# Forty warming matmuls of 32 columns in place of five of 256 columns, ahead of a retention layer and two MLPs

## The chip, the core and the metric

The kernel runs on one core of one Trainium2 chip. The metric is the device time of one execution in microseconds (us). Three runs of the kernel before took 884.5, 882.04 and 884.17 us, with a median of 884.17 us. One more execution was profiled: it took 882.56 us, and its span, from its first to its last instruction, is 880.8 us.

## The reference

The input is a set of queries, keys and values for 4 batches, 8 heads, 576 positions and a head size of 64. Three layers follow one another, all in float32:

```python
scores = q @ k.T / 8                              # per batch and head
ret    = scores * where(i >= j, gamma[h] ** (i - j), 0)
x      = (ret @ v) heads side by side             # 2304 tokens x 512
h      = x @ w_in                                 # 512 x 2048
x      = (h * sigmoid(h)) @ w_out                 # 2048 x 512
h      = x @ w2_in
out    = (max(h, 0) ** 2) @ w2_out
```

The first two lines are a retention layer (attention with a decaying mask in place of the softmax); the two pairs of matrix products behind it are MLPs with the same sizes and different gates.

## The kernel before, in words

The 2304 tokens are cut into 18 units of 128 tokens for the retention layer and into five blocks of 512, 384, 384, 512 and 512 tokens for the MLPs. A unit is two chunks of 64 positions. The retention is computed chunk by chunk with a running state of 64 x 64 per head: for each unit, `scores` makes the products of queries and keys (line 257) and the products of keys and values that go into the state (line 262); `mask` multiplies the first by the decay (line 266, on VectorE); `new_state` adds to the state (lines 295 and 297, on VectorE) and lets GpSimd decay it (line 301); `scale_q` scales the queries on GpSimd (line 274); `prep_k` scales the keys, one half on GpSimd (line 244) and one half on ScalarE (line 247); `values` makes the output from the state and the masked scores (lines 312 to 328), and ScalarE copies a part of it out (line 330). Its matmuls are plain float32 with a tile of 64 x 64, and each is two instructions in the trace, with a weight load (`LDWEIGHTS`) each.

The MLP matmuls (`mm3`, line 74) split every number into a high and a low part and multiply three of the four pairs, in fp32r, one instruction and one weight load each. The weights come in over SyncE's queue and are split by ScalarE and VectorE (`conv_a` to `conv_d`, lines 101 to 125).

The order on each engine is the order in which the program is written; nothing reorders it. At the front, `first_units` writes out by hand how the first four retention units and the split of the first weights interleave on all engines. The first MLP matmul needs units 0 to 2, that is, the low part that line 350 makes of unit 2's output. Behind it stands one long loop of MLP work in which the other 14 units of the retention are spread.

Ahead of `first_units`, the kernel sets a tile `zero` to zero on GpSimd (line 535), takes a PSUM tile `warm`, and multiplies zeros by zeros `WARM` times into it (lines 537 and 538). Nothing reads `warm`. These matmuls stand first in TensorE's queue; the first `scores` stands right behind them and waits for its input, which SyncE's queue begins to load at 0.74 us. The weight tile of a warming matmul is 128 x 128, and its moving tile is 256 columns wide.

Of the kernel before, what the change touches and what calls it, by code (L numbers as in the profile page):

```python
# [31 lines left out]
W2_LAG, W2_NUM, W2_DEN = 0, 9, 8  # L32
HALF = (slice(0, 64), slice(64, 128))
RAW = 3
WARM = 5


@with_exitstack
def kernel(
# [16 lines left out]
    nc = tc.nc  # L56
# [12 lines left out]
    mm = nc.tensor.matmul  # L69
# [135 lines left out]
    def att_psum(startup, name):  # L205
        pool, tag = ps_a, "a"
        if startup:
            pool, tag = [(ps_a, "a"), (ps_s, "s"), (ps_s, "s"), (ps_s, "s")][ps_n[0] % 4]
            ps_n[0] += 1
        return pool.tile([128, 2, 512], F32, tag=tag, name=name)  # L210
# [321 lines left out]
    nb = len(BLOCKS)  # L532
    u_end = [sum(BLOCKS[: j + 1]) // C for j in range(nb)]
    zero = wp.tile([128, 1024], F32, tag="w", name="zero")
    nc.gpsimd.memset(zero[:, 0:256], 0.0)
    warm = att_psum(True, "warm")
    for _ in range(WARM):
        mm(warm[:, 0, 0:256], zero[:, 0:128], zero[:, 0:256], start=True, stop=True)
    nc.vector.memset(dummy, 0.0)
    nc.scalar.activation(dummy, dummy, ACTF.Silu)  # L540
    load_consts(0)
# [129 lines left out]
```

## Time and profile before

| what | value |
|---|---|
| median of three runs | 884.17 us |
| the profiled execution | 882.56 us |
| its span | 880.8 us |
| TensorE busy with matmuls | 857.8 us, 97% of the span, 5954 instructions |
| VectorE, ScalarE, GpSimd busy | 43%, 41%, 6% |
| mean granted TensorE clock | 0.988 of full |

The engines are PE (TensorE's matmuls), PEld (its weight loads, which overlap matmuls), DVE (VectorE), ACT (ScalarE), POOL (GpSimd) and SP (SyncE, whose queue issues most transfers). A granted clock of 1.00 is 2.4 GHz and 0.50 is 1.2 GHz; before the first event of the clock on record the views show 1.00 all the same. Busy times of matmuls are modelled, since matmuls are pipelined: the distance from one start to the next (called the pitch below) tells more than the duration of one. In rows with several instructions merged, the second number is the time from the start of the first to the end of the last.

### The profile page before, as it was taken

The numbers are of one execution on the slowest core, as the hardware profiler recorded it, in microseconds if no ns is written. First come the engines' busy times: TensorE is split into PE (matmuls) and PEld (weight loads), VectorE is DVE, ScalarE is ACT, GpSimd is POOL, SyncE is SP. The second block draws the span as 40 slices with busy tenths as digits, with TensorE's granted clock in tenths as the row PEclk, the third lists the DMA queues.
The fourth block names the chain that finished last, engine by engine and source line by source line (L and its number), as shares of the span: only waits on it lengthen the run. The fifth ranks groups of instructions, "written<-read, shape, count | busy, mean of one in ns | idle before, by whom it ended". The sixth has DMA issues, their size and how long they took to land.

```text
span 880.8 us, 14140 instructions
## 1 busy us (share of the span) xinstructions
PE 857.8 (97%) x5954; PEld 741.2 (84%) x5954; DVE 379.2 (43%) x642; ACT 357.0 (41%) x722; POOL 50.3 (6%) x73
## 2 busy tenths in 40 slices
PE   6799999999999999999999999999999999999998
PEld 5777778999999888888888888899999888888886
DVE  5699992221322222215666777432233332323222
ACT  4588872333334333326565656322222222222221
POOL 4211101000210111000000000000000000000000
PEclk7999999999999999999999999999999999999999
DMA  9455641111211213004433542020020010001001
GB/s 352 148 169 206 217 144 48 49 49 49 85 49 52 82 49 121 1 1 152 136 96 104 180 129 78 0 84 1 1 84 1 1 67 17 1 1 48 1 1 48
DMA packets 21663, 68.27 MB, mean 78 GB/s; under 512 B 2400, under 2 KB 4192, under 8 KB 21216
## 3 DMA queue, kind: packets, MB, share of 16 engines
q1 hardware_dynamic: 16272, 54.14, 17.8%
q10 hardware_dynamic: 5328, 13.24, 4.2%
q8 instruction: 46, 0.75, 0.4%
q14 instruction: 17, 0.14, 0.1%
HBM read 57.93 MB, written 9.44 MB: 76 GB/s over the span
## 4 chain that ended last, share of the span: by engine, by line
PE 84%; DVE 0%; DMA 0%; ACT 0%; issue 0%; SPq 0%
PE acc L74 41%; PE ph L74 40%; PE Q L312 2%; PE P L257 1%; PE P L262 1%; DMA raw<-att 0%; ACT raw L247 0%; DVE gl L466 0%; PE Q L328 0%; DVE Q L345 0%; DVE xl L350 0%; DVE wl L125 0%; ACT xh L348 0%; ACT wh L121 0%; DVE y L508 0%
## 5 line engine op out<-in xcount | busy, mean ns | idle before, releaser
L74 PE MATMUL ph<-xh,wh 128*128 128x512 f32 (+2 forms) x648 | 239.2, 369 | 4.9 <-ACT xh L348 1.9
L74 PE MATMUL ph<-xl,wh 128*128 128x512 f32 (+2 forms) x648 | 237.6, 367 | 0.3 <-DVE xl L350 0.3
L74 PE MATMUL ph<-xh,wl 128*128 128x512 f32 (+2 forms) x648 | 237.8, 367 | 0.0
L466 DVE TENSOR_TENSOR gl<-sg,gh 128x512 fp32r<-128x512 f32 (+1 forms) x160 | 101.8, 637 | 185.2 <-ACT gh L465 185.2
L74 PEld LDWEIGHTS ph<-xh,wh 128*128 128x128 f32 x648 | 121.9, 188 | 22.9 <-ACT sg L458 2.3
L461 DVE SCALAR_TENSOR_TENSOR sg<-ph,sg 128x512 f32<-128x512 f32 (+1 forms) x80 | 51.0, 638 | 198.4 <-ACT sg L460 198.4
L74 PEld LDWEIGHTS ph<-xl,wh 128*128 128x128 f32 x648 | 122.0, 188 | 16.4 <-DVE xl L350 0.5
L74 PEld LDWEIGHTS ph<-xh,wl 128*128 128x128 f32 x648 | 122.0, 188 | 14.7
L460 ACT ACTIVATE sg<-ph 128x512 f32<-128x512 f32 (+1 forms) x80 | 44.5, 556 | 211.7 <-PE ph L74 210.9
L74 PE MATMUL acc<-gh,wh 128*128 128x512 f32 (+1 forms) x320 | 119.5, 374 | 0.0
L74 PE MATMUL acc<-gl,wh 128*128 128x512 f32 (+1 forms) x320 | 117.9, 369 | 0.9 <-DVE gl L466 0.9
L74 PE MATMUL acc<-gh,wl 128*128 128x512 f32 (+1 forms) x320 | 117.7, 368 | 0.0
L458 ACT ACTIVATE sg<-ph 128x512 f32<-128x512 f32 (+1 forms) x80 | 44.3, 554 | 179.3 <-PE ph L74 178.6
L465 ACT CAST gh<-sg 128x512 fp32r<-128x512 f32 (+1 forms) x160 | 92.3, 577 | 53.2 <-DVE sg L461 50.6
L74 PE MATMUL acc<-wh,gl 128*128 128x512 f32 x288 | 112.7, 391 | 0.0
L74 PE MATMUL acc<-wl,gh 128*128 128x512 f32 x288 | 112.6, 391 | 0.0
L74 PE MATMUL acc<-wh,gh 128*128 128x512 f32 x288 | 112.0, 389 | 0.0
L74 PEld LDWEIGHTS acc<-gl,wh 128*128 128x128 f32 x320 | 60.2, 188 | 8.8 <-DVE gl L466 1.5
L74 PEld LDWEIGHTS acc<-gh,wh 128*128 128x128 f32 x320 | 60.3, 188 | 8.5
L74 PEld LDWEIGHTS acc<-gh,wl 128*128 128x128 f32 x320 | 60.2, 188 | 7.5
L74 PEld LDWEIGHTS acc<-wh,gl 128*128 128x128 f32 x288 | 54.0, 188 | 11.4
L74 PEld LDWEIGHTS acc<-wh,gh 128*128 128x128 f32 x288 | 54.1, 188 | 10.5
(50 smaller groups left out, 697.1 us busy)
## 6 DMA issues: line engine op xcount, KB each, us to landing
wr<-w SPq DMA_DIRECT2D x64, 512.0 KB, 3.5
raw<-att SPq DMA_DIRECT2D x32, 512.0 KB, 4.5
x<-y ACTq DMA_DIRECT2D x12, 256.0 KB, 4.3
xr<-x ACTq DMA_DIRECT2D x3, 1024.0 KB, 4.9
out<-y SPq DMA_DIRECT2D x10, 256.0 KB, 2.2
out<-y ACTq DMA_DIRECT2D x7, 256.0 KB, 2.3
x<-y ACTq DMA_DIRECT2D x8, 192.0 KB, 1.9
xr<-x ACTq DMA_DIRECT2D x2, 768.0 KB, 4.3
```

Of the source, the lines that this page charges most:

```text
L74: mm(o, a, b, start=first and i == 0, stop=last and i == n - 1)
L257: mm(o, dims(u, a, e, b, 768), dims(u, a, e, b, 0), start=True, stop=True)
L262: mm(o, toks(u, a, e, b, 256), toks(u, a, e, b, 512), start=True, stop=True)
L312: mm(w, a, b, start=e not in started, stop=last)
L458: nc.scalar.activation(s, ph, ACTF.Silu)
L460: nc.scalar.activation(s, ph, ACTF.Relu)
L461: nc.vector.scalar_tensor_tensor(s, ph, 0.0, s, op0=ALU.max, op1=ALU.mult)
L465: nc.scalar.copy(gh, s)
L466: later.append(lambda: nc.vector.tensor_sub(gl, s, gh))
```

## The change

The count of warming matmuls goes from 5 to 40 and the columns of each from 256 to 32. The memset ahead of them covers 128 columns, those that the weight tile needs, in place of 256. Nothing else differs.

```diff
-WARM = 5
+WARM = 40
...
     zero = wp.tile([128, 1024], F32, tag="w", name="zero")
-    nc.gpsimd.memset(zero[:, 0:256], 0.0)
+    nc.gpsimd.memset(zero[:, 0:128], 0.0)
     warm = att_psum(True, "warm")
     for _ in range(WARM):
-        mm(warm[:, 0, 0:256], zero[:, 0:128], zero[:, 0:256], start=True, stop=True)
+        mm(warm[:, 0, 0:32], zero[:, 0:128], zero[:, 0:32], start=True, stop=True)
```

## Rows read from the trace of the kernel before

**Rows 1.** The page: busy time by engine; chain that ended last, by engine.

```profile
PE 857.8 (97%) x5954; PEld 741.2 (84%) x5954; DVE 379.2 (43%) x642; ACT 357.0 (41%) x722; POOL 50.3 (6%) x73
...
PE 84%; DVE 0%; DMA 0%; ACT 0%; issue 0%; SPq 0%
```

**Rows 2.** Busy time in four stretches from 40 to 120 us, their sum.

```profile
sum 80.00, PE 77.15 PEld 61.64 DVE 73.01 ACT 65.34 POOL 8.48; mean PE 19.29 PEld 15.41 DVE 18.25 ACT 16.34 POOL 2.12
```

**Rows 3.** Timeline of the front: start, length, engine, line, operation, idle before it and releaser.

```profile
1.10 4.57 PE L538 MATMUL warm<-zero 128*128 128x256 f32 x10 [1.10 <-POOL zero L535]
...
6.72 0.81 PE L257 MATMUL P<-raw 64*64 64x64 f32 x32 [1.05 <-DMA raw<-att]
...
9.89 1.48 PE L262 MATMUL P<-raw 64*64 64x64 f32 x32 [2.37 <-POOL raw L244]
...
12.54 0.68 DVE L266 TENSOR_TENSOR rf<-P,cs 128x512 f32<-128x512 f32 x1
...
14.94 0.99 DVE L109 SCALAR_TENSOR_TENSOR t<-wr,t 128x512 int32<-128x512 int32 x1
...
15.85 0.41 DVE L297 TENSOR_TENSOR S<-P,dS 128x256 f32<-128x256 f32 x1
...
16.91 1.86 POOL L274 TENSOR_TENSOR raw<-raw,cs 128x256 f32<-128x256 f32 x2
...
18.74 0.61 POOL L244 TENSOR_TENSOR raw<-raw,cs 128x256 f32<-128x256 f32 x1
...
19.40 1.35 PE L262 MATMUL P<-raw 64*64 64x64 f32 x30 [1.16 <-POOL raw L244]
...
23.14 0.37 ACT L330 COPY xs<-Q 128x256 f32<-128x256 f32 x1 [3.14 <-PE Q L328]
...
25.05 0.43 DVE L107 TENSOR_SCALAR t<-t 128x512 int32<-128x512 int32 x1 [3.12 <-ACT t L101]
...
33.45 0.41 PE L74 MATMUL ph<-xh,wh 128*128 128x384 f32 x1 [1.53 <-DVE xl L350]
```

**Rows 4.** Two stretches of the front: length, busy by engine, PEclk, DMA share, GB/s.

```profile
15.30:18.30 3.00, 2.94 (x110) 2.75 (x102) 2.52 (x5) 0.89 (x2) 2.04 (x4) 0.50 1.02 406
...
19.40:23.10 3.70, 3.70 (x119) 3.64 (x121) 2.12 (x5) 0.60 (x3) 3.01 (x5) 0.57 1.03 411
```

**Rows 5.** The tile warm: shortest, median, longest duration in ns, first and last start.

```profile
L538 PEld LDWEIGHTS warm<-zero x10: 285/337/337, 1.1 to 4.7; 128*128 128x128 f32 x10
L538 PE MATMUL warm<-zero x10: 574/634/792, 1.1 to 5.1; 128*128 128x256 f32 x10
```

**Rows 6.** Timeline of PE, 36.4 to 40.5 us: third and last of 24 short matmuls.

```profile
37.86 0.27 PE L74 MATMUL ph<-xh,wl 128*128 128x128 f32 x1
...
40.21 0.28 PE L74 MATMUL ph<-xh,wl 128*128 128x128 f32 x1
```

**Rows 7.** Groups of weight loads, mean ns behind the bar: 37.7 to 40.2; 135.3 to 138.5 us.

```profile
L74 PEld LDWEIGHTS ph<-xh,wh 128*128 128x128 f32 x8 | 1.5, 192 | 0.0
...
L74 PEld LDWEIGHTS ph<-xh,wh 128*128 128x128 f32 x2 | 0.7, 330 | 0.0
```

**Rows 8.** Timeline of PE: scores of unit 1; later values and scores at full clock.

```profile
16.29 1.06 PE L262 MATMUL P<-raw 64*64 64x64 f32 x29
...
91.54 1.09 PE L312 MATMUL Q<-raw,S 64*64 64x64 f32 x30
...
93.09 0.50 PE L74 MATMUL ph<-xh,wh 128*128 128x512 f32 x1
...
107.97 0.69 PE L257 MATMUL P<-raw 64*64 64x64 f32 x32
...
109.07 0.50 PE L74 MATMUL acc<-gh,wh 128*128 128x512 f32 x1
```

**Rows 9.** The page: DMA queue, packets, MB, share; timeline of PE at 26 us.

```profile
q8 instruction: 46, 0.75, 0.4%
...
26.23 1.02 PE L262 MATMUL P<-raw 64*64 64x64 f32 x28 [2.66 <-issue]
```

## The prediction

> **What bounds the kernel now.** I read the page first: TensorE is busy for 97% of the span, and 84% of the chain of waits is TensorE's [rows 1]. Then I asked whether a delay at the front is ever given back. From 40 to 120 us TensorE is busy for 77.15 of 80 us and VectorE for 73.01 [rows 2], so no engine has room to catch up, and behind that TensorE has next to no gap. A microsecond at the front is taken as a microsecond at the end.
>
> So the front decides: the time until the first MLP matmul, which starts at 33.45 us [rows 3]. The reader is to see in its timeline which wait ends last at each step. The warming matmuls run from 1.10 to 5.67 us. The first scores then wait 1.05 us for their input, start at 6.72, and their second half waits 2.37 us more for GpSimd, until 9.89. TensorE is early here: unit 0's scores end at 11.37, and their reader, the mask of line 266, starts at 12.54, behind earlier work in VectorE's queue. From the mask the chain goes on without a gap worth naming: VectorE to line 109 (14.94) and line 297 (15.85), GpSimd through line 274 (16.91) and line 244 (18.74), TensorE's state products at 19.40 and unit 1's values behind them, ScalarE's copy at 23.14 that waited 3.14 us for them, VectorE's line 107 at 25.05 that waited 3.12 us in turn, and VectorE up to 33.45. From mask to first MLP matmul that is 33.45 - 12.54 = 20.9 us.
>
> The clock matters in this stretch. It is 0.50 from 15.3 to 18.3 us, and 0.57 on average from 19.4 to 23.1, where TensorE is on the chain [rows 4].
>
> **The change, part by part.** *Removed:* ten matmul instructions with ten weight loads, 4.57 us in all [rows 3, 5]. Their pitch is (5.1 - 1.1) / 9 = 0.44 us, and the load (337 ns) hides behind the matmul.
>
> *The memset:* 128 columns for 256; TensorE started 1.10 us after the span's start, and I take 0.1 us off that (bounds 0 and 0.3).
>
> *Added:* 40 matmuls are 80 matmul instructions and 80 weight loads. The columns are as many as before (40 x 32 = 5 x 256), so the streaming alone would cost the same 4.57 us. But each of the 80 loads brings a full 128 x 128 tile and no longer has a long matmul to hide behind. The trace has such a case: 24 MLP matmuls of 128 columns, each with a load of 128 x 128. From the third, at 37.86 us, to the last, at 40.21, are 21 steps, so the pitch is 0.112 us [rows 6], at a granted clock of 1.00. Matmuls still shorter cannot run ahead of the same loads, so 0.112 us is the pitch at full clock.
>
> The warming matmuls don't start at full clock. Their loads take 337 ns [rows 5]; a load of the same size takes 192 ns at 1.00 and 330 ns just after 135.3 us, where the clock is 0.50 [rows 7]. The front thus begins at 0.50, although its records hold no event, and I estimate the pitch there as twice 0.112, 0.224 us. Bounds for all 80: 8.9 us with every one at full clock, and 80 x 0.337 = 27 us were loads to run strictly one after the other. The nearest row is the one of a chain of loads that overlap short matmuls, so I take that pitch.
>
> Now the fork: does the clock come up while they run? In the kernel before, it came up late in 4.57 us of unbroken matmuls or just behind them: the last warming matmul still starts at the old pitch, at 5.1 us, and the scores at 6.72 run 32 instructions in 0.81 us [rows 3, 5], where 29 take 1.06 at 0.50 [rows 8]. The new ones stream 32 columns where a load streams 128, so the array multiplies for a quarter of the time and loads for the rest. Where TensorE was busy 2.94 of 3.00 us with short matmuls [rows 4], after gaps, the clock stayed at 0.50. It came up only near 22.6 us (the mean of 0.57 over 3.70 us makes 0.5 us of full clock), after three more microseconds of work. No row shows a stretch made of loads. I think it likelier that loading doesn't raise the clock than that it does.
>
> **The sum.** 80 x 0.224 = 17.9 us from 1.0: the warming ends at 18.9 us. Scores of unit 0 have their data long before, and stand behind it in the queue. At 0.50, 29 of the 32 instructions of half a unit's scores take 1.06 us [rows 8], and two halves overlap a little, so one unit takes some 2.05; they end at 20.95, and the mask starts at 21.05 in place of 12.54: +8.5 us. Nothing else of the front can use the wait: behind the mask in VectorE's queue, behind line 244 in GpSimd's and behind unit 0's copy in ScalarE's stands work that needs unit 0. So the 20.9 us from mask to MLP follow, less what the clock gives: state products and values of unit 1 ran from 19.40 to 23.1, 3.6 us; at full clock they are 0.6 (half of 109.07 - 107.97) and 1.55 (93.09 - 91.54) [rows 3, 8], so between 0 and 1.45 us are saved. I take half, 0.75. Total +7.75 us on the profiled execution's 882.56 us: **890.3 us**, with bounds of this case from 888.5 (clock up in all of that stretch, warming 1 us shorter) to 892 (none of it, and loads half a microsecond to one slower in all). The profiled execution lies 1.6 us under the median of the runs (884.17), about the spread of the three, and I don't correct for it.
>
> **A rule that speaks against this.** The Trainium skill, "TensorE: Matmul & The Clock Gate", Part 1 (the HAM clock gate), says that warming up costs an amount of time and not a number of matmuls. By it forty short ones would raise the clock just as five long ones did, and the time would be that of the first rival, about 883 us. The trace agrees for long ones alone; no run here shows it for short ones.
>
> **Rivals.** *1. The clock comes up during the warming (no measurable change).* Say at 5.5 us, between the two bounds above. Then (5.5 - 1.0) / 0.224 = 20 pairs run at 0.50 and 60 at full clock, 60 x 0.112 = 6.7 us, and the warming ends at 12.2. Scores at full clock take 1.1 us [rows 8], and the mask starts at 13.4, +0.9 us. If the clock then holds until 23 us, the 1.45 us above come back: -0.6 in sum. So 882.0 to 883.5, 883 as one number. It decides the case from the point where the warming ends before about 11.3 us (12.54 less 1.2): from there on it costs nothing at all. For it: the rise in the kernel before, after 4 us of work. Against it: the array's idle cycles.
>
> *2. As 1, and an instruction fetch gets onto the chain (slower, within 0.3%).* 46 packets brought 0.75 MB of instructions [rows 9], 16 KB each, for 2 x 5954 instructions: about 256 per packet. Before 26.23 us TensorE stood for 2.66 us with nothing that it waited for. By the program's order that is behind 10 warming matmuls, 64 + 48 + 64 + 64 + 96 of the units and some 34 of unit 3's scores, 380 matmuls with 380 loads: 760, about three packets' worth. VectorE's queue hid it. 140 more instructions at the front move that border to some 620, which is in the middle of unit 1's values at about 21 us, on the chain. Cost 0 to 1.5 us, as the packet is asked for earlier too: 883 to 885. The Trainium skill, "Runtime: NRT & Kernel Launch", Instruction fetch mechanics, calls such borders mostly hidden; this trace shows one of 2.66 us that VectorE's work alone hid.
>
> *3. Columns alone set the pace.* If loads of the same tile cost nothing, the warming takes 4.57 us again: 882.6. Against it: the loads of 337 ns hid behind matmuls of 256 columns [rows 5]; an eighth of those columns would have to hide the same load.
>
> **How the numbers follow.** A measurement of this kernel can tell about 0.3%, 2.65 us, from no change. Forecast 0.52; rival 1 0.27; rival 2 0.11; rival 3 0.05; 0.05 for a front that comes out faster than any of these (clock up from 12 us on and no stop of TensorE). The forecast is slower by over 0.3% (+7.75), as are 0.04 out of rivals 1 and 2 with a late rise; rivals 1 to 3 are otherwise within. That gives 0.05 faster, 0.39 same, 0.56 slower. Cases of both kinds hold much of the chance, so the range goes from rival 1's low end to the forecast's high one, 881.8 to 892; the forecast's own is 888.5 to 892.
>
> **What would show it.** Right: 80 loads on the tile `warm` with a pitch of 0.22 us to the end, the first scores at about 18.9 us, the mask of line 266 at 21, the first MLP matmul near 41, and from there the same distances as before. Wrong in the fork: a pitch that drops to 0.11 us on the way, scores at 12 to 13 us, and the first MLP matmul at 33 to 35. Wrong in the pace: `warm` done at 6 us. Wrong in the carrying: a first MLP matmul that is late and an end that is not.

## Result and the profile after

The changed kernel takes 889.63 us (median of four runs, 888.52 to 890.84), the kernel before 883.65 us in the same comparison (882.04 to 884.5). The ratio is 1.008, 95% interval 1.0057 to 1.0102: slower by 6 us as the difference of the medians. The profiled execution took 888.52 us, 5.96 us more than the one profiled before; its span is 886.7 us. The ratios in this document leave out a single execution of 952.98 us (without warming, at a mean granted clock of 0.848), and they are not quotients of the two medians, from which they differ by up to about 0.1%.

The timeline of the front after the change, to be laid beside [rows 3] (start, length, engine, line, operation, idle before it and releaser):

```profile
0.99 17.27 PE L538 MATMUL warm<-zero 128*128 128x32 f32 x80 [0.99 <-POOL zero L535]
...
18.19 1.13 PE L257 MATMUL P<-raw 64*64 64x64 f32 x32
19.10 1.08 PE L262 MATMUL P<-raw 64*64 64x64 f32 x32
...
20.25 0.69 DVE L266 TENSOR_TENSOR rf<-P,cs 128x512 f32<-128x512 f32 x1 [7.72 <-PE P L262]
...
27.11 0.99 PE L262 MATMUL P<-raw 64*64 64x64 f32 x31 [1.33 <-POOL raw L244]
...
29.63 0.37 ACT L330 COPY xs<-Q 128x256 f32<-128x256 f32 x1 [1.91 <-PE Q L328]
...
31.55 0.43 DVE L107 TENSOR_SCALAR t<-t 128x512 int32<-128x512 int32 x1 [2.06 <-ACT t L101]
...
39.98 0.66 PE L74 MATMUL ph<-xh,wh 128*128 128x384 f32 x1 [0.52 <-DVE xl L350]
```

The reader is to compare starts. The warming ends at 18.26 us in place of 5.67. The first scores no longer wait for their input; they wait in TensorE's queue. VectorE, which reached the mask of line 266 without a wait before, now stands still for 7.72 us ahead of it and starts it at 20.25 in place of 12.54: +7.71 us. From there the distance shrinks: +6.49 at line 330's copy, +6.50 at line 107, +6.53 at the first MLP matmul.

The tile `warm`, as in [rows 5] (durations in ns, first and last start):

```profile
L538 PEld LDWEIGHTS warm<-zero x80: 285/333/333, 1.0 to 17.8; 128*128 128x128 f32 x80
L538 PE MATMUL warm<-zero x80: 401/401/419, 1.0 to 17.9; 128*128 128x32 f32 x80
```

79 steps lie between 0.99 and 17.86 us; behind the first, which takes 0.23 us, each takes 0.213 or 0.214, so the pitch is 0.2133 us to the end. The shortest load (285 ns) is the first one; after it all take 333 ns, as loads of this size do at 0.50 [rows 7], so the clock never came up under them.

### The profile page after: what moved, and what is told of

The parts are those of the page before. It is cut to its first block, busy times and chain, and to the rows that moved or that the text cites. A ratio compares the mean times of both kernels' runs of the same rounds, so it can differ in the third digit from the quotient of the medians.

```text
span 886.7 us, 14280 instructions
## 1 busy us (share of the span) xinstructions
PE 867.9 (98%) x6024; PEld 752.5 (85%) x6024; DVE 379.2 (43%) x642; ACT 357.0 (40%) x722; POOL 49.4 (6%) x73
## 4 chain that ended last, share of the span: by engine, by line
PE 84%; DVE 0%; DMA 0%; ACT 0%; issue 0%; SPq 0%
PE acc L74 40%; PE ph L74 40%; PE Q L312 2%; PE P L257 1%; PE P L262 1%; DMA raw<-att 0%; ACT raw L247 0%; DVE gl L466 0%; PE Q L328 0%; DVE Q L345 0%; DVE xl L350 0%; DVE wl L125 0%; ACT xh L348 0%; ACT wh L121 0%; DVE y L508 0%
## 5 line engine op out<-in xcount | busy, mean ns | idle before, releaser
L74 PEld LDWEIGHTS acc<-wl,gh 128*128 128x128 f32 x288 | 54.1, 188 | 10.6
```

The costliest lines, as they stand in the source:

```text
L74: mm(o, a, b, start=first and i == 0, stop=last and i == n - 1)
```

## Experiments

Theory: each pair of load and matmul is paced by the load of its 128 x 128 tile, 0.2133 us at a clock of 0.50; the clock did not come up because the matmuls between the loads were so short; what makes the mask of line 266 late is carried to the end. Rivals: a pair costs its time by being issued, whatever its tile; the clock would stay down whatever is streamed; the front gives time back; or the old warming had a worth that was lost. Each of the seven kernels below was compared with the kernel before on the same chip; that one's median was 882.13 us in the first four comparisons and 882.01 in the last three. The diffs are against the changed kernel.

**A narrow weight tile.**

```diff
-        mm(warm[:, 0, 0:32], zero[:, 0:128], zero[:, 0:32], start=True, stop=True)
+        mm(warm[0:32, 0, 0:32], zero[:, 0:32], zero[:, 0:32], start=True, stop=True)
```

> The changed kernel with a weight tile of 32 columns in place of 128; 80 matmuls of 32 columns as before. Theory (the load of the 128 x 128 tile paces each pair): a load of a quarter of the columns takes a quarter of 0.213 us, so the pitch falls to 0.05 to 0.07 us, the warming ends at 5.5 to 6.5 us, ahead of the input of the first scores, and the time is that of the kernel before, 882 to 885 us. Rival (a pair of instructions costs its 0.21 us whatever its tile, by being issued): pitch 0.21 us, first scores at 18 us, 888.5 to 891 us.

882.37 us, ratio 1.001 (0.9998 to 1.0023). The tile `warm` and the first PE rows in its timeline:

```profile
L538 PEld LDWEIGHTS warm<-zero x80: 113/157/159, 1.0 to 4.9; 128*32 128x32 f32 x80
L538 PE MATMUL warm<-zero x80: 196/241/260, 1.0 to 5.0; 128*32 128x32 f32 x80
```

```profile
0.99 4.17 PE L538 MATMUL warm<-zero 128*32 128x32 f32 x80 [0.99 <-POOL zero L535]
7.01 0.81 PE L257 MATMUL P<-raw 64*64 64x64 f32 x32 [1.85 <-DMA raw<-att]
```

As many instructions and the same 32 columns of the moving tile, and the pitch is (5.0 - 1.0) / 79 = 0.05 us, about a quarter of 0.2133. The whole 6 us is gone. The columns of the weight tile set the price; being issued does not.

This run shows something else that was not asked of it. Its clock came up during the warming: the first rise on record is at 4.59 us, and the last loads take 113 ns where the median is 157. So matmuls of 32 columns are not too short for a rise by themselves; they were so behind loads of 128 columns.

**More columns behind the same loads.**

```diff
-        mm(warm[:, 0, 0:32], zero[:, 0:128], zero[:, 0:32], start=True, stop=True)
+        mm(warm[:, 0, 0:128], zero[:, 0:128], zero[:, 0:128], start=True, stop=True)
```

> The changed kernel with 128 columns streamed by each of the 80 matmuls in place of 32; the loads are the same 80 of 128 x 128. Theory (loads pace, and the clock stayed at 0.50 because the matmuls between the loads were so short): the pitch begins at 0.21 us as in the changed kernel, the clock comes up after some 4 to 7 us, the pitch falls to 0.11 us, the warming ends at 11 to 13.5 us, and the time is 882 to 886 us. Rival (the streaming has nothing to do with the clock): the pitch is 0.21 us to the end, the first scores start at 18 us or later, 888.5 to 891 us.

886.08 us, ratio 1.0038 (1.0025 to 1.0051): the mechanism as expected, the time 0.08 us above the range given. Three stretches of it (length; PE busy and the number of its instructions in the stretch, then the same for PEld, DVE, ACT and POOL; clock, DMA share, GB/s), and then its timeline, PE but for the DVE row:

```profile
1.00:5.20 4.20, 4.20 (x19) 4.20 (x20) 0.00 (x0) 1.22 (x2) 0.00 (x0) 1.00 0.69 221
5.20:12.20 7.00, 7.00 (x66) 6.88 (x69) 2.12 (x4) 5.06 (x14) 0.82 (x1) 1.00 1.04 399
...
35.30:39.30 4.00, 4.00 (x13) 4.00 (x14) 3.22 (x7) 1.44 (x3) 0.00 (x0) 0.50 0.01 4
```

```profile
12.11 0.69 PE L257 MATMUL P<-raw 64*64 64x64 f32 x32
...
13.34 0.69 DVE L266 TENSOR_TENSOR rf<-P,cs 128x512 f32<-128x512 f32 x1 [0.59 <-PE P L262]
...
23.46 0.37 PE L312 MATMUL Q<-raw,S 64*64 64x64 f32 x2 [1.45 <-issue]
```

Until 5.2 us, 19 matmuls start in 4.2 us; behind it 61 take 6.8, 0.11 us each. The clock column shows 1.00 in the first two rows, since no event is on record before the rise; the pitch is what shows the level (0.2133 is 1.2 GHz here, 0.112 is 2.4 GHz). Four times the columns cost nothing while the loads pace, and with them the clock came up after 4.2 us, where 32 columns left it down for 17.3 us. The warming ended at 12.2 us and the mask was late by 0.8 us, where the prediction's first rival had 12.2 and 0.9; that rival's time, 883 us, did not come of it. The last row is a stop of TensorE without a releaser in the middle of unit 1's values: the second rival, with 1.45 us. The first MLP matmul starts at 35.26 us, 1.8 us later than in the kernel before. What is left of the 0.4% fits the clock, which fell again: from 35.3 to 39.3 us, 13 of the first MLP matmuls take 4.0 us at 0.50, where the kernel before ran them at 1.00.

**Half the count.**

```diff
-WARM = 40
+WARM = 20
```

> The changed kernel with 20 warming matmuls (40 pairs) in place of 40. Theory (the warming costs only what makes the mask of line 266 late): it ends at 1.0 + 40 x 0.2133 = 9.5 us, scores of unit 0 end near 11.7, the mask starts at 12.4 to 12.8 as in the kernel before, and the time is 882 to 885 us. Rival (each pair costs its share wherever it stands): half of the 6 us, 886.6 us.

883.03 us, ratio 1.0003 (0.9993 to 1.0014). Its timeline, PE and the mask on DVE:

```profile
0.99 8.74 PE L538 MATMUL warm<-zero 128*128 128x32 f32 x40 [0.99 <-POOL zero L535]
9.66 1.13 PE L257 MATMUL P<-raw 64*64 64x64 f32 x32
...
12.36 0.68 DVE L266 TENSOR_TENSOR rf<-P,cs 128x512 f32<-128x512 f32 x1
```

Forty pairs delay the first scores by 3 us and the mask by nothing. The price is not proportional: it begins where TensorE is no longer early.

**No warming.**

```diff
-    zero = wp.tile([128, 1024], F32, tag="w", name="zero")
-    nc.gpsimd.memset(zero[:, 0:128], 0.0)
-    warm = att_psum(True, "warm")
-    for _ in range(WARM):
-        mm(warm[:, 0, 0:32], zero[:, 0:128], zero[:, 0:32], start=True, stop=True)
+    ps_n[0] = 1        # the PSUM tiles rotate as before
```

> No warming matmuls and no memset at all. Theory (in the kernel before, TensorE was early in the front, and the clock that the warming raised fell again before any step that was waited for): the mask of line 266 starts at 12.4 to 12.8 us as before, 882 to 885 us. Rival (the five warming matmuls of the kernel before were worth something, and a part of what the change lost is their effect): 886 us or more.

882.76 us, ratio 1.0002 (0.9993 to 1.0011). VectorE's mask, and TensorE's stop in unit 3's scores:

```profile
12.55 0.68 DVE L266 TENSOR_TENSOR rf<-P,cs 128x512 f32<-128x512 f32 x1
...
26.27 0.59 PE L262 MATMUL P<-raw 64*64 64x64 f32 x16 [2.42 <-issue]
```

The five warming matmuls of the kernel before were worth nothing that can be measured, so nothing of the 6 us is a lost benefit.

**Twice the count.**

```diff
-WARM = 40
+WARM = 80
```

> The changed kernel with 80 warming matmuls (160 pairs) in place of 40. Theory (the front is the chain, and what it loses is carried to the end one to one): the 80 further pairs cost 80 x 0.2133 = 17.1 us, the mask of line 266 starts at 37.3 us, and the time is that of the changed kernel plus 17, less or more 1.5 for where the clock falls and rises: 904 to 908 us. Rival (a part of a delay at the front is given back behind it): under 903 us.

906.2 us, ratio 1.0282 (1.0269 to 1.0295). The tile `warm`, then the mask on DVE:

```profile
L538 PE MATMUL warm<-zero x160: 401/401/421, 1.0 to 34.9; 128*128 128x32 f32 x160
```

```profile
37.31 0.69 DVE L266 TENSOR_TENSOR rf<-P,cs 128x512 f32<-128x512 f32 x1 [24.36 <-PE P L262]
```

Eighty further pairs moved the mask by 17.06 us (20.25 to 37.31). The time over the kernel before is 24.2 us here, against 6.0 and 9.3 in the two comparisons of the changed kernel, so 15 to 18 us more. A delay of the front is not given back. And 34 us of such pairs did not raise the clock either: the pitch is 0.213 us to the end.

**Matmuls in TensorE's gaps, none at the front.**

```diff
-WARM = 40
+WARM = 0          # and the loop taken out as above, with zero kept
...
+    FILL = {("P", 2): 3, ("P", 3): 4, ("Q", 0): 4}
+    def fill(what, u, o):
+        for _ in range(FILL.get((what, u), 0)):
+            mm(o, zero_t[0][:, 0:128], zero_t[0][:, 0:128], start=True, stop=True)
...
+        fill("P", u, P[:, 0, 256:384])    # scores: between lines 257 and 262
...
+        fill("Q", u, Q[:, 1, 256:384])    # values: ahead of line 312
```

> No warming at the front; 11 matmuls of 128 columns on zeros stand in TensorE's gaps instead: four ahead of unit 0's values, three and four between the two halves of the scores of units 2 and 3. Theory (of all the front, TensorE's clock matters where unit 1's values are waited for): the clock is at 1.00 from some 17 us on, unit 1's values end 1.2 us earlier than in the kernel before, and 1 to 2 us come off its time, 880 to 882.5 us where the kernel before has 882 to 884. Rival (the matmuls in the gaps delay what stands behind them, or the clock falls again): no difference, or slower by 1 us.

883.67 us, ratio 1.0023 (1.0013 to 1.0033): no gain, slower by 0.2%. The attempt at a version better than both kernels failed. Its timeline of PE, and the count of its instructions until its two stops (PE and PEld in brackets):

```profile
16.66 0.82 PE L255 MATMUL P<-zero 128*128 128x128 f32 x5
20.01 0.38 PE L255 MATMUL P<-zero 128*128 128x128 f32 x1 [2.53 <-issue]
```

```profile
0.00:18.00 18.00, 8.14 (x221) 7.20 (x221) 7.60 (x13) 9.51 (x23) 6.13 (x12) 1.00 0.90 341
0.00:24.80 24.80, 12.54 (x348) 11.35 (x348) 11.19 (x20) 11.84 (x32) 11.33 (x20) 0.93 0.91 349
```

TensorE stood for 2.53 us with nothing that it waited for, ahead of the second half of unit 2's scores, and ran that half at the low level again (32 instructions in 1.03 us from 20.32). Theory failed at this place; what these stops are is told below.

**The changed kernel again.** No edit.

> The changed kernel once more, for another profile of it and more times. Theory (the delay of the first scores is fixed by the loads, and the spread of the times comes from where the clock falls and rises): the warming again ends within 0.1 us of 18.3 us and the mask of line 266 starts at 20.25 us; the stretches at 0.50 behind it lie elsewhere, and the time is 888 to 891 us. Rival (the first trace was one of several ways in which the warming can go): the clock comes up in the warming, and the time is under 886 us.

891.33 us (four runs, 889.19 to 891.96), ratio 1.0108 (1.0094 to 1.0123). The tile `warm` answers line for line (80 matmuls, 1.0 to 17.9, 401 ns) and the mask starts at 20.25 us again. The stretches at 0.50 lie elsewhere: 36.5 to 39.9 and 142.3 to 145.7 us, where the first profile had 35.2 to 42.0 and none near 140. Theory held; the median is 0.3 us above the range given.

## Why the prediction was right

The forecast was 890.3 us, and 889.63 was measured. That it came within 0.7 us is partly luck: it put +7.75 us on an execution of 882.56 us, and measured were +5.98 us on a median of 883.65 us, so a rise that was 1.8 us too large met a base that was 1.1 us too low. In the second comparison the rise was 9.3 us on 882.01 us. What the runs bear out is the mechanism, and a rise of 6 to 9 us. Step by step:

- *The pace.* 0.224 us was estimated for a pair, as twice the 0.112 us at full clock, and 0.2133 measured, 1.9 times as much. With 17.27 us in place of 17.9, the first scores start at 18.19 in place of 18.9. That the load's columns make the price is shown by the narrow tile.
- *The fork.* The clock stayed at 0.50, as the likelier branch had it. Two runs show that it hung on so few columns streamed behind so wide a load: with 128 columns behind the same loads the clock rose after 4.2 us, and with the same 32 columns behind loads of 32 it rose 3.6 us after the first matmul. The rule of the Trainium skill, "TensorE: Matmul & The Clock Gate", Part 1, that warming up costs an amount of time and not a number of matmuls, does not carry that far: 17.3 us of short matmuls behind wide loads, and 34 us in the run with twice the count, raised nothing in this case.
- *The mask.* +8.5 us was forecast, +7.71 measured: the pace explains 0.6 of the difference.
- *Unit 1's values.* 0.75 us was allowed for a clock that might be up (0 to 1.45); 1.2 came back: [rows 3] have 23.14 - 12.54 = 10.60 us from mask to copy, the timeline after has 29.63 - 20.25 = 9.38. All of it lies between the start of line 262 (19.40, then 27.11 us: still +7.71) and the copy, and the clock there was 1.00, with its rise on record at 24.93 us, where it was 0.57 before [rows 4]:

```profile
27.10:29.60 2.50, 2.49 (x119) 2.44 (x122) 2.14 (x5) 0.62 (x3) 1.79 (x3) 1.00 0.02 7
```

- *The carrying.* One to one was forecast, with the same distances as before from the first MLP matmul on. The run with twice the count bears out the first; the second did not hold: two terms that the sum did not have are in the profile and in part cancel. The first MLP matmuls ran at 0.50 until 42.0 us, where the kernel before ran them at 1.00, and a stretch at 0.50 near 135 us, which the kernel before had behind a wait, did not come. Starts of the same three matmuls, first in the kernel before, then in the changed one:

```profile
34.57 0.33 PE L74 MATMUL ph<-xh,wh 128*128 128x384 f32 x1
...
135.65 0.52 PE L74 MATMUL ph<-xh,wh 128*128 128x384 f32 x1
...
138.42 0.48 PE L74 MATMUL acc<-gh,wl 128*128 128x512 f32 x1
```

```profile
42.03 0.34 PE L74 MATMUL ph<-xh,wh 128*128 128x384 f32 x1
...
142.94 0.33 PE L74 MATMUL ph<-xh,wh 128*128 128x384 f32 x1
...
144.44 0.40 PE L74 MATMUL acc<-gh,wl 128*128 128x512 f32 x1
```

The distance is 6.53 us at the first MLP matmul, 7.46 at the first pair here, 7.29 at the second and 6.02 at the third, and 5.96 at the end. The clock, over the stretches in which it differs (columns as in the run with 128 columns), in the kernel before and then in the changed one:

```profile
33.50:35.50 2.00, 2.00 (x12) 2.00 (x13) 1.90 (x4) 0.00 (x0) 0.00 (x0) 1.00 0.31 121
135.20:138.60 3.40, 3.40 (x12) 3.21 (x11) 0.36 (x1) 0.76 (x2) 0.00 (x0) 0.50 0.00 0
```

```profile
40.00:42.00 2.00, 2.00 (x6) 2.00 (x7) 1.90 (x4) 0.00 (x0) 0.00 (x0) 0.50 0.03 8
142.00:145.40 3.40, 3.40 (x18) 3.14 (x19) 0.85 (x2) 1.33 (x3) 0.00 (x0) 1.00 0.00 0
```

So the sum 8.5 - 0.75 = 7.75 became 7.7 - 1.2 + 0.9 - 0.2 - 1.3 = 5.9. The second profile of the changed kernel has its low stretches elsewhere and ends 6.6 us behind the kernel before. That where they fall makes much of the spread between executions is likely, and not shown: of the eight of the changed kernel, the three shortest (888.52 to 889.19 us) have a mean granted clock of 0.995 or 0.996, the next two (890.56 and 890.84) 0.994, the three longest (891.22 to 891.96) 0.993 or 0.992.

- *An error in the working of the second rival.* Unit 1's values are 64 matmul instructions and not 96, so the border that the text put at some 760 instructions lies at 10 + 64 + 48 + 64 + 64 + 64 + 34 = 348 matmuls and as many loads, 696. The mechanism stands, and the run with 128 columns puts the stop in unit 1's values, where the text had it. In the changed kernel itself the border was reached at 28.7 us, with the transfers of the front done (a DMA share of 0.02 in the row above), and TensorE did not stop.

## What to carry to other kernels

Matmuls that only warm the engine were priced here by the larger of two things, the columns they stream and the columns of the weight tile they load (behind loads of 128 columns at 0.50, a pitch of 0.21 us with 32 or 128 columns streamed and 0.43 with 256); cutting the first and multiplying the count buys loads. Before tuning such a block, look for how early the engine behind it is: here it had some 5 us to spare, within which five long ones, twenty short ones and none made no difference, and each microsecond beyond it made the mask late by as much; the end was late by that, less or more what the clock then gave or took. The clock that the five long ones raised was worth nothing here: it was at 0.50 again by 15.3 us [rows 4], ahead of unit 1's values, for which the chain waits.

## What the runs showed of the hardware that was not expected

TensorE's stops without a releaser, at the front of these kernels, come after a fixed number of its instructions, whatever the program does there. Instructions until the stop (PE and PEld in brackets), in the kernel before, without warming, and with 128 columns:

```profile
0.00:24.50 24.50, 15.57 (x347) 13.60 (x348) 11.12 (x20) 12.31 (x34) 11.42 (x20) 0.72 0.93 353
```

```profile
0.00:24.50 24.50, 11.60 (x348) 10.95 (x348) 11.12 (x20) 12.20 (x34) 11.10 (x19) 1.00 0.92 353
```

```profile
0.00:22.50 22.50, 16.98 (x348) 16.29 (x348) 11.03 (x20) 11.15 (x28) 8.37 (x17) 0.99 0.92 352
```

It is 348 matmuls and 348 loads each time (in the kernel before, the 348th matmul starts only behind the stop). The other stops without a releaser in these traces, two with the narrow tile, one with 128 columns, one with half the count, one with filled gaps:

```profile
21.91 0.27 PE L312 MATMUL Q<-raw,S 64*64 64x64 f32 x2 [0.38 <-issue]
26.25 0.33 PE L312 MATMUL Q<-raw,S 64*64 64x64 f32 x4 [0.91 <-issue]
...
17.05 0.27 PE L257 MATMUL P<-raw 64*64 64x64 f32 x2 [0.92 <-issue]
...
22.90 0.63 PE L257 MATMUL P<-raw 64*64 64x64 f32 x27 [1.22 <-issue]
...
26.09 0.32 PE L263 MATMUL P<-raw 64*64 64x64 f32 x2 [1.67 <-issue]
```

With those shown above they are nine, in six kernels, and all come after 221, 348 or 475 matmuls and as many loads, give or take one: borders 127 pairs apart, that is 254 instructions, where a packet of 16 KB brings about 256 [rows 9]. The packets are on record in the DMA view; here is its line for the kernel before from 23.69 to 23.71 us, for 128 columns from 20.93 to 20.95, and for the changed kernel from 29.30 to 29.33 (a share over so short a stretch means nothing):

```profile
q8 instruction: 1, 0.02, 342.2%
...
q8 instruction: 1, 0.02, 322.5%
...
q8 instruction: 1, 0.02, 199.6%
```

The first stop ends at 26.23 us, the second at 23.46, each 2.5 us after the packet's start; over all nine stops it is 2.4 to 2.6 us. Where the packet started 2.8 us or more before TensorE reached the border, there was no stop. What differs is when the packet starts. In the kernel before it does so 3.95 us after the border ahead of it was passed (19.75 us), at a DMA share near 1; in the changed kernel, at a time when the transfers were done, 0.6 us after (28.7 us). So a stop of 0.38 to 2.66 us is a packet that came late. That the transfers of the front held it up fits these starts, but is not shown: in the run with twice the count one packet started as much as 2.4 us after the border ahead of it, with a DMA share of 0.00, and no run took the transfers away by themselves. The Trainium skill, "Runtime: NRT & Kernel Launch", Instruction fetch mechanics, calls the cost of such a border mostly hidden; at a front full of transfers it was not, and a TensorE made faster there ran into the border sooner.
